# Engine order from a list scheduler, scores by head pair, transposes in the hT ring: a banded attention followed by a squared-ReLU MLP on one Trainium2 core

## Chip, cores, metric

One core of one Trainium2 chip. The metric is the device time of one execution in microseconds (us), the median of several runs. A "span" is the time from the first to the last instruction of the one profiled execution; it is some 1.8 us shorter than the same execution as timed (266.5 against 268.28 us for the kernel before).

Engines: PE does matmuls, PEld loads their stationary operand, DVE and ACT work on tensors, POOL issues most loads here (the prediction calls them SWDGE loads), SP the stores.

Names in the profiles: `tr`, `trq`, `trk`, `trx` are transposes on PE; `qz` is q transposed, with the two heads of a pair kept apart by zeros, `kT` is k transposed; `sc` are scores, `esc` their exp, `at` that times the mask; `po` is the attention output, `x` the same normalised, `xT` its transpose; `hT`, `hr`, `hs` are the hidden layer before the relu, after it, and squared; `acc` are the output accumulators and `o` the copy of one that is stored ("eviction"); `win` and `wout` are the weights. PE shows two rates here: eight `hT` matmuls last 1.04 us at the full rate and about 1.9 us at the half rate.

## The reference

```python
# q, k, v: (4, 8, 768, 64); n_global 8, n_local 96
scores = scale * q @ k.T + bias            # bias: -slope[h] * distance
keep   = is_global | is_local              # first 8 keys, and the last 96
a      = softmax(where(keep, scores, -1e9))
x      = (a @ v).transpose(0, 2, 1, 3).reshape(3072, 512)
out    = relu(x @ w_in) ** 2 @ w_out       # w_in (512, 2048), w_out (2048, 512)
```

There are 24 tiles of 128 rows, six per batch. As keys reach back 96 rows only, a tile needs its own keys and those of the tile before. Two tiles make a block of 256 rows for the MLP: 12 blocks, each in 8 steps of 256 hidden columns, 96 steps in all.

## The kernel before

All eight banks of PSUM, the buffers for matmul results, are used (the prediction cites the page for the number): two for the output accumulators `acc`, two for `hT`, two for one score tile `sc`, one for transposes `tr`, one for attention outputs `po`. The order of instructions on each engine is that in which Python emits them, by a hand-made table of times:

```python
def unit_a(j):                       # transposes of q and k, both into ONE bank
    if j < NPLAIN:                   # the two fp32 "plain" tiles: cast by DVE first
        nc.vector.tensor_copy(q_sb[j], plain["q", j])
        nc.vector.tensor_copy(k_sb[j], plain["k", j])
    tr = ps_tr.tile([P, 2 * NPAIR, P], BF16, name="tr", tag="tr")
    # ... four transposes of q, four of k
    nc.vector.tensor_copy(z[:D, :, 0, :], tr[:D, :NPAIR, :])
    nc.vector.tensor_copy(z[D:, :, 1, :], tr[D:, :NPAIR, :])
    nc.scalar.copy(kT[j], tr[:, NPAIR:, :])
# unit_scores: 4 matmuls into a tile of two banks, one exp and one multiply of 1024
# unit_pv: 8 small matmuls into po, then reciprocal and normalisation on DVE
# unit_f: 4 transposes of x into the tr bank, copied to xT by ACT

def stage1(g):                       # 8 matmuls into hT, relu on ACT, square on DVE
    ...
def stage2(g):                       # 4 matmuls into acc[0], acc[1]
    ...
    if s == NSTEP - 1:               # end of a block: evict and store
        for sub in range(2):
            nc.scalar.copy(o, acc[blk][sub])
            nc.sync.dma_start(out=out[r : r + P, :], in_=o)

put(0, A=-9, B=-8.9, D=-8.6, E=-8.4, F=-8.3)      # ... a line per early tile
for g in range(-1, NG + DELAY):
    if 0 <= g < NG:
        stage1(g)
    while pos < len(when) and when[pos][0] < g + 1:
        _, j, u = when[pos]
        UNITS[u](j)
        pos += 1
    if g - DELAY >= 0:
        stage2(g - DELAY)
```

The softmax here doesn't subtract the row's maximum and nothing guards it: scores larger than these inputs give would overflow.

## Time and profile before

| | before |
|---|---|
| time, median of 3 runs | 268.24 us |
| span of the profiled run | 266.5 us |
| PE stream (all matmuls by their start-to-start) | 212.3 us |
| first hT matmul | 26.7 us |
| PE idle for the o copy of a block | 10.5 us, 9 times |

The group lines read: source line, engine, operation, output <- inputs, shapes, count, then busy us and mean ns of one, then how long the engine stood idle just before these and for whom. The lines themselves stand in the prediction.

### The profile page before, as it was taken

To read this page: it belongs to the slowest core of one execution; us is meant where nothing else is said; L and a number is where in the kernel's file an instruction comes from. 1 tells how busy PE (TensorE), PEld (TensorE's weight loads), DVE (VectorE), ACT (ScalarE), POOL (GpSimd) and SP (SyncE) were. 2 spreads that over 40 slices of the span, in tenths; PEclk is the share of its full clock that TensorE was granted. 3 is DMA by queue.
4 is the path that set the end of the run, shared out by engine and by line. 5 is a ranking of instruction groups with operands and counts; after the bars stand their busy time and mean duration, and the time that the engine had idled before them with its cause. 6 is when DMAs were issued, how large, how long until landed. Compare 5 with 4: busy or idle time off the path is not lost.

```text
span 266.5 us, 4844 instructions
## 1 busy us (share of the span) xinstructions
PE 223.3 (84%) x1935; PEld 160.3 (60%) x1968; DVE 151.1 (57%) x350; ACT 139.8 (52%) x229; POOL 73.4 (28%) x94
## 2 busy tenths in 40 slices
PE   1345969686989899899799899898998998999993
PEld 1124657464666677577577677576676775766641
DVE  6444576466457576565557567565575675653310
ACT  5432474444557456556556555654745646635321
POOL 8986778999994000000000000000000000000000
PEclk9999999999999999999999999999999999999999
DMA  8999999999999300200200200200200200202022
GB/s 161 155 196 200 186 180 155 157 155 155 198 157 154 87 2 0 81 1 2 79 2 1 79 2 0 81 0 2 79 2 1 79 2 1 81 0 81 0 79 79
DMA packets 84758, 20.76 MB, mean 78 GB/s; under 512 B 75520, under 2 KB 81664, under 8 KB 84736
## 3 DMA queue, kind: packets, MB, share of 16 engines
q0 software_dynamic: 77120, 13.11, 63.2%
q1 hardware_dynamic: 7616, 7.34, 8.3%
q8 instruction: 15, 0.25, 0.4%
q14 instruction: 7, 0.06, 0.1%
HBM read 27.26 MB, written 6.29 MB: 126 GB/s over the span
## 4 chain that ended last, share of the span: by engine, by line
PE 66%; DVE 16%; ACT 11%; issue 5%; ACTq 0%
PE acc L338 27%; PE hT L314 26%; PE sc L219 7%; DVE hs L325 4%; ACT hr L323 4%; DVE x L275 3%; DVE qz L188 2%; ACT esc L228 2%; PE po L265 2%; ACT o L349 2%; PE trx L291 2%; DVE qz L187 2%; ACT kT L189 2%; DVE at L237 1%; DVE rs L274 1%
## 5 line engine op out<-in xcount | busy, mean ns | idle before, releaser
L325 DVE TENSOR_TENSOR hs<-hr 128x512 bf16<-128x512 f32 x96 | 66.3, 691 | 69.6 <-ACT hr L323 69.3
L338 PE MATMUL acc<-wout,hs 128*128 128x512 bf16 x351 | 92.9, 379 | 12.3 <-ACT o L349 10.5
L314 PE MATMUL hT<-xT,win 128*128 128x256 bf16 x768 | 101.2, 276 | 0.1
L314 PEld LDWEIGHTS <-win 128*128 128x128 bf16 x768 | 75.7, 99 | 28.2 <-issue 0.2
L323 ACT ACTIVATE hr<-hT 128x512 f32<-128x512 f32 x96 | 57.7, 601 | 54.6 <-PE hT L314 54.6
L338 PEld LDWEIGHTS <-hs 128*128 128x128 bf16 x384 | 35.7, 98 | 37.6 <-issue 13.2
L228 ACT ACTIVATE esc<-sc 128x1024 bf16<-128x1024 f32 x44 | 45.2, 1028 | 5.8 <-PE sc L219 4.7
L237 DVE TENSOR_TENSOR at<-esc,E 128x1024 bf16<-128x1024 bf16 x44 | 30.4, 691 | 27.1 <-ACT esc L228 27.0
L189 ACT COPY kT<-tr 128x512 bf16<-128x512 bf16 x24 | 14.0, 584 | 50.8 <-DVE qz L188 45.1
L219 PE MATMUL sc<-qz,kT 128*128 128x256 bf16 x160 | 25.8, 287 | 7.5 <-ACT kT L189 5.2
L87 POOL DMA_DIRECT2D v<-in_v_dram x24 | 23.4, 975 | 2.6 <-DMA win<-in_moe_w_in_dram 1.2
L96 POOL DMA_DIRECT2D k<-in_k_dram x22 | 21.3, 968 | 3.3 <-DMA wout<-in_moe_w_out_dram 2.8
L219 PEld LDWEIGHTS <-kT 128*128 128x128 bf16 x160 | 15.3, 102 | 10.6 <-ACT kT L189 6.1
L96 POOL DMA_DIRECT2D q<-in_q_dram x22 | 21.2, 965 | 1.4 <-DMA win<-in_moe_w_in_dram 0.7
L275 DVE TENSOR_TENSOR x<-po,rs 128x256 bf16<-128x256 f32 x48 | 20.4, 425 | 1.7
L265 PE MATMUL po<-v,at 128*128 128x65 bf16 x320 | 16.8, 196 | 3.4 <-DVE x L275 3.4
L265 PEld LDWEIGHTS <-at 128*128 128x128 bf16 x320 | 15.1, 100 | 5.7 <-DVE x L275 4.9
L349 ACT COPY o<-acc 128x512 f32<-128x512 f32 x24 | 13.0, 597 | 6.3 <-PE acc L338 6.3
L180 PE MATMUL tr<-ident,q 128*128 128x128 bf16 x96 | 9.9, 230 | 6.8 <-DVE q L175 6.8
L294 ACT COPY xT<-trx 128x512 bf16<-128x512 bf16 x24 | 14.0, 582 | 3.1 <-PE trx L291 3.1
L291 PE MATMUL trx<-ident,x 128*128 128x128 bf16 x96 | 9.9, 226 | 5.7 <-ACT kT L189 4.1
L291 PEld LDWEIGHTS <-x 128*128 128x128 bf16 x96 | 7.5, 100 | 6.9 <-issue 4.5
(34 smaller groups left out, 94.2 us busy)
## 6 DMA issues: line engine op xcount, KB each, us to landing
out_dram<-o SPq DMA_DIRECT2D x24, 256.0 KB, 2.2
v<-in_v_dram POOLq DMA_DIRECT2D x24, 128.0 KB, 6.1
q<-in_q_dram POOLq DMA_DIRECT2D x22, 128.0 KB, 5.9
k<-in_k_dram POOLq DMA_DIRECT2D x22, 128.0 KB, 6.0
win<-in_moe_w_in_dram POOLq DMA_DIRECT2D x8, 256.0 KB, 7.2
wout<-in_moe_w_out_dram POOLq DMA_DIRECT2D x8, 256.0 KB, 9.8
plain_q<-in_q_dram SPq DMA_DIRECT2D x2, 256.0 KB, 3.9
plain_k<-in_k_dram SPq DMA_DIRECT2D x2, 256.0 KB, 4.3
```

What stands on the lines that cost most here:

```text
L87: nc.gpsimd.dma_start(out=v_sb[j][:, :, :D], in_=v[b, :, t * P : (t + 1) * P, :].rearrange("h p d -> p h d"),)
L96: nc.gpsimd.dma_start(out=dst.rearrange("p (h d) -> p h d", h=H), in_=src[b, :, rows, :].rearrange("h p d -> p h d"),)
L219: nc.tensor.matmul(out=sc[:, pi, i * 2 * P : (i + 1) * 2 * P], lhsT=kT[kj][:, pair, :], rhs=z[:, pair, :, :], start=True, stop=True, skip_ ...
L228: nc.scalar.activation(out=esc, in_=sc.rearrange("p a b -> p (a b)"), func=Act.Exp, scale=scale)
L237: nc.vector.tensor_mul(at, esc, bias)
L265: nc.tensor.matmul(out=po[:, hi, :], lhsT=a4[:, hi // 2, i, hi % 2, :], rhs=v_sb[kj][:, h, :], start=(i == 0), stop=(i == 1), skip_group_c ...
L275: nc.vector.tensor_tensor(out=x[:, 4 * hf : 4 * hf + 4, :], in0=po[:, :, :D], in1=rs.to_broadcast([P, 4, D]), op=Alu.mult,)
L291: nc.tensor.transpose(out=trx[:, kt, :], in_=x[:, kt * P : (kt + 1) * P], identity=ident)
L314: nc.tensor.matmul(out=hT[:, c, :], lhsT=w_in_sb[s][:, kt, c * P : (c + 1) * P], rhs=xT[blk][:, kt, :], start=(kt == 0), stop=(kt == KM - ...
L323: nc.scalar.activation(hr, hT, Act.Relu)
L325: nc.vector.tensor_mul(hs, hr, hr)
L338: nc.tensor.matmul(out=acc[blk][sub], lhsT=hs[:, c, sub * P : (sub + 1) * P], rhs=w_out_sb[s][:, c, :], start=(s == 0 and c == 0), stop=(s ...
```

## The change

The intent is that PE never waits. The hand table goes; every piece of work is registered with its costs, dependencies and buffer rings, and a list scheduler emits all in the order in which they could start. Scores are made one head pair at a time, in two buffers of one bank. Transposes of q, of k and of x each take a bank out of the hT ring, which grows to three (those of the first two tiles take one of the accumulators' banks). Copies out of PSUM go to ACT or DVE, whichever is free earlier in the plan. The two plain tiles, the first two of q and k, are transposed in fp32 without a cast. Some buffers outside PSUM grow too (`qz` from 3 to 4, `hs` from 10 to 14), and the last block finishes one accumulator before the other.

```diff
+class Plan:
+    LAG = {"PE": 0.25, "ACT": 0.15, "DVE": 0.12, "SP": 2.6, "POOLQ": 2.5, "DMA": 0.0}
+    ...                              # picks the op and engine with the earliest start
-    DELAY = 8
+    NACC = 2
+    NQ, NKT, NQZ = 10, 2 * TPB, 4
-    ps_acc = ... bufs=1              # two tags
-    ps_h   = ... bufs=2
-    ps_sc  = ... bufs=1              # tiles of two banks
-    ps_tr  = ... bufs=1
+    ps_acc = ... bufs=NACC           # one tag
+    ps_h   = ... bufs=5 - NACC       # three, shared with the transposes
+    ps_sc  = ... bufs=2              # tiles of one bank
...
+    clock = [6.0]                    # assumed landing: 0.85 us a load, 1.3 a weight
-            nc.sync.dma_start(       # plain q and k
+    for n, src, eng in (("q", q, nc.sync), ("k", k, nc.scalar)):
+            eng.dma_start(
...
-    for j in range(NT):
-        nc.vector.memset(v_sb[j][:, :, D : D + 1], 1.0)
     (qz memsets, mask work)
+    for j in range(NT):
+        nc.vector.memset(v_sb[j][:, :, D : D + 1], 1.0)
...
-    for s in range(NSTEP):
-        load_w_in(s)
     for s in range(NSTEP):
+        load_w_in(s)
         load_w_out(s)
...
+                z = plan.op(("z", e_, j), {"DVE": 0.43, "ACT": 0.57}, emit_z,
+                            deps=[tr] + qz_users[zi], key=base + 0.1)
...
-    when.sort()                      # and the loop over steps
+    for o in plan.run():
+        if o["emit"]:
+            o["emit"](o["engine"])
```

## The prediction

> **What bounds the kernel now.** I read the page first (busy shares, slices, groups), then PE's waits by stretch, the chain of waits over one steady block, and the timeline of the start and of the end.
>
> ```profile
> span 266.5 us, 4844 instructions
> PE 223.3 (84%) x1935; PEld 160.3 (60%) x1968; DVE 151.1 (57%) x350; ACT 139.8 (52%) x229; POOL 73.4 (28%) x94
> ...
> PE   1345969686989899899799899898998998999993
> ...
> L338 PE MATMUL acc<-wout,hs 128*128 128x512 bf16 x351 | 92.9, 379 | 12.3 <-ACT o L349 10.5
> ```
>
> PE is the bound, but 84% is not its rate: matmuls overlap, so I price them by start-to-start. In the timeline eight hT matmuls run from 251.32 to 252.19 (0.866 us, 108 ns each) and four acc matmuls from 250.45 to 251.32 (216 ns each). In the same way four scores take 0.44 us (109 ns), four transposes 0.222 (55.5 ns), eight po 0.245 (31 ns). The stream alone needs: hT 768 x 0.1083 = 83.2; acc 384 x 0.2165 = 83.1; sc 176 x 0.109 = 19.2; transposes 288 x 0.0555 = 16.0; po 352 x 0.031 = 10.9. Sum 212.4 us. So 54 of the 266.5 us are not PE streaming. Where are they?
>
> The start. Before the first hT matmul PE has streamed only 32 transposes, 16 scores, 24 po, 4.3 us:
>
> ```profile
> 4.52 0.61 PE L180 MATMUL tr<-ident,q 128*128 128x128 bf16 x4 [4.52 <-DVE q L175]
> ...
> 11.98 0.61 PE L180 MATMUL tr<-ident,q 128*128 128x128 bf16 x4 [2.25 <-DVE q L175]
> ...
> 26.66 1.89 PE L314 MATMUL hT<-xT,win 128*128 128x256 bf16 x8
> ```
>
> The reader sees that tile 1's transposes wait until 11.98, though its data is there early (longest plain landing 4.8 us after an issue at 2.82): DVE casts it behind tile 0's work. The first hT stands at 26.66: 26.7 - 4.3 = 22.4 us lost. The end: the last acc matmul starts at 262.0, so ends near 262.4, and copy and store take 4.1 us. Left for the middle: 54.1 - 22.4 - 4.1 = 27.6 us. PE's waits from 94 to 226, then from 26.7 to 94:
>
> ```profile
> PE acc L338 <- ACT o L349: 9.0, 7, 1.4
> ```
>
> ```profile
> PE sc L219 <- ACT kT L189: 3.6, 4, 1.0
> PE po L265 <- DVE x L275: 2.6, 4, 1.2
> PE trx L291 <- ACT kT L189: 2.5, 2, 1.7
> PE sc L219 <- ACT esc L228: 1.4, 2, 1.1
> PE acc L338 <- ACT o L349: 1.2, 1, 1.2
> ```
>
> In the steady part one wait is all there is, once in a block of eight steps. The chain of waits at such a boundary shows what holds the eviction:
>
> ```profile
> 107.19 0.69 DVE hs L325
> 108.01 0.42 DVE x L275
> 108.43 0.32 DVE qz L187
> 108.77 0.44 DVE qz L188
> 109.49 0.28 issue
> 109.77 0.60 ACT o L349
> 110.41 1.08 PE acc L338 x4
> ```
>
> The o copy itself is 0.60 us, but on ACT's queue it stands behind the kT copy, which waits for both qz copies of DVE (they share its source bank), which wait behind hs and x. A cross-queue knot, not a lack of ACT or DVE time (52% and 57% busy). The acc starts at 110.41, 129.36, 148.75 give a block of 19.4 us (18.95 with a first tile). Its stream is 8 x 1.732 + 2 tiles x 2.03 = 17.9 (17.2): 1.5 to 1.7 us lost per block, of which 1.2 to 1.45 is this wait.
>
> **What the Trainium skill says.** "TensorE: Matmul & The Clock Gate", Back-to-back issue gap, gives N/2.4 + 2.5 ns warm: 109 and 216 ns for 256 and 512 columns; the trace agrees (108, 216). It also gives a loaded figure of 131 ns at 512, which this trace does not reach. Part 1 of that page has the array at half rate until about 3.4 us of sustained work. The page's clock row shows 9s throughout, but in the chain the first hT groups take 1.71 and 1.72 us for eight, against 0.87 later: the durations agree. "PSUM — Partial Sum Buffer", Specifications, gives 8 banks of 2 KiB per partition: before uses 2 acc + 2 hT + 2 sc + 1 tr + 1 po, after 2 + 3 + 2 + 1, full both times, so the third hT bank is paid with the tr bank. No view shows banks. "Perfetto Trace Analysis", DVE / Act Engine Instruction, says each instruction pays a fixed bubble: exp of 1024 takes 1028 ns and relu of 512 takes 601, so 427 per half and about 174 fixed (estimate from both rows).
>
> **The change part by part.** From the built order of both kernels, the number of PE matmuls is the same; the stream stays 212.4.
>
> 1. Scores in pairs. 44 exps become 80 of 512 and 16 of 256 columns: by the split above 80 x 0.60 + 16 x 0.39 = 54 instead of 45.2 us. The multiplies: 1024 bf16 take 691 ns as 512 fp32 do, so the halves cost about 0.42 (estimate): 80 x 0.42 + 16 x 0.29 = 38 instead of 30.4. With copies now spread (ACT gets 24 qz, 20 kT, 17 xT, 12 o; DVE 24 qz, 4 kT, 7 xT, 12 o), ACT comes to hr 57.7 + 54 + 73 copies x 0.58 = 42 + masks 5.5, about 160 us, DVE to about 165. Both under 70% of the new span. The price lies beside PE.
>
> 2. The block boundary. In the new order the two o copies are split between ACT and DVE, and between a block's last acc and the next block's first stand transposes, one hT group and one score pair: 0.22 + 0.87 + 0.22 = 1.3 us of PE work, over an eviction of 0.6. kT no longer shares a bank with q's transposes, so it doesn't wait for qz. The 1.2 to 1.45 us goes; I keep 0.3 a block for slips. Seven blocks from 91 to 226 gain about 8 us.
>
> 3. The start. fp32 transposes straight from the plain tiles, no cast; q and k issued on two queues; the score pairs pipeline through exp and multiply. Against it: the memsets of v now stand after four qz memsets (0.52 each), an identity copy and the mask work (1.0), so DVE reaches v's first memset near 4.8 us, and POOL's first v load, issued at 2.96 before, waits for it. All SWDGE loads shift by about 1.9 us. k of tile 3, issued at 8.38 before, now near 10.2, lands about 6 us later, at 16.3 (median of that row). Then, cold: transpose 0.6, po 0.5, norm 0.65, po 0.5, norm 0.65, trx 0.7, xT 0.5, and the queueing of tile 1's last exps: first hT near 21 us. By then PE has streamed 40 transposes, 20 scores and 24 po: 5.1 us. 207.3 remain (208.1 before). The start gains 26.7 - 21 - 0.8 = about 5 us.
>
> 4. The ramp. Loads now go win, wout in turn. The bytes up to the last wout are the same, and it landed at 41.65 before (a later k load waits for it there); at the queue's 1.4 us per weight and 0.7 per load this gives, shifted, q of tile 4 near 29, win 5 near 34.5, q of tile 5 near 36.6, win 7 near 42. PE, from 21, reaches these places near 28, 34, 36 and 43: about 2 us of waits. Before, the ramp (26.7 to 91) lost some 16 us: 27.6 less 7 x 1.5 and about 1 at the end. It has the 11.3 us of listed waits, the half clock (about 3), and drains. With three hT banks, two score buffers and o, qz, kT no longer in one knot I expect: half clock 2.5, loads 2, queue order 3.5 (ACT has 14 relus, 11 exps and 5 copies in these first 21 us of PE stream, 18 us, so it is tight there).
>
> 5. The end. The last block finishes one acc early, but the other still needs copy and store: 4.1 us stays.
>
> Sum: 21 + 207.3 + 8 (ramp) + 2.5 (steady) + 0.5 (last block) + 4.1 = 243.4 us of span, 1.7 more as timed (266.5 span, 268.24 timed): 245. The allowances are more likely too big than too small, as before's steady waits are almost one kind alone; I put 243.
>
> **The rivals.** (a) The bank ring turns into the new wait: 96 hT groups and 72 transposes take turns in three banks, seven takings per four steps. For it: a transpose's two copies may sit on two queues. Against: the tightest place, hT group after q and k transposes and four acc, has 1.5 us from the earlier group's end, over a relu of 0.60 plus 0.2 of drain. If wrong by 0.3 us a step: 96 x 0.3 = +29, no gain left. (b) ACT or DVE becomes the bound in the ramp or queues in fixed order wait on each other, since the scheduler's durations are guesses: +5 to 10, 250. (c) Late loads: the order was fixed on assumed landings some 3 us earlier than my estimate; PE stops in order. Against: PE too runs later. +3 to 5. (d) It runs as dense as planned with hardly a wait: 21 + 207.3 + 4 + 4.1 + 1.7 = 238, or 236 if the first hT comes at 19.
>
> **Range and chances.** 243 us; 236 (rival d) to 251 (b) eight times in ten. Within 2% (above 262.9) would need rival (a) at 0.2 us a step: chance 0.03; slower 0.01; faster 0.96.
>
> **What would show it.** Right: first hT at 20 to 22 us; L338's wait for the o copy all but gone; blocks of 17.9 to 18.3 us; ACT near 160 and DVE near 165 us busy; PE's waits gathered before 45 us. Wrong: hT or transposes waiting for relu or copies each step (a); PE waiting for exps or kT after 45 us (b); matmuls released by DMA (c).

## The result, and the profile after

The changed kernel takes 235.92 us (235.41 to 236.87, 4 runs) against 268.18 us. The ratio is 0.8798, interval 0.8761 to 0.8834: 12% faster. The forecast was 243 (236 to 251): the direction and most of the size were right, but the time fell just under the range.

The page of the changed kernel, its counterparts of the lines shown for before:

```profile
span 235.1 us, 4992 instructions
...
PE 219.5 (93%) x1968; PEld 159.1 (68%) x1968; DVE 153.8 (65%) x399; ACT 149.8 (64%) x282; POOL 73.8 (31%) x94
...
PE   1768699999999999999999999999999999999992
...
L629 PE MATMUL acc<-wout,hs 128*128 128x512 bf16 x384 | 101.1, 379 | 0.8 <-DVE hs L598 0.8
```

PE reads 9 in every slice from the sixth to the last but one, and the acc group's wait for the o copy is gone. ACT and DVE are busier, as foreseen (150 and 154 us). All waits of PE in the whole run (columns: who waited for whom, us in total, times, longest):

```profile
PE trq L327 <- DVE v L215: 4.8, 1, 4.8
PE hT L565 <- DMA win<-in_moe_w_in_dram: 1.9, 3, 1.4
PE trq L327 <- DMA q<-in_q_dram: 1.7, 3, 0.7
PE po L466 <- DVE x L492: 1.1, 2, 0.8
PE trq L327 <- DVE kT L266: 0.8, 1, 0.8
PE acc L629 <- DVE hs L598: 0.8, 2, 0.6
PE trk L327 <- DMA k<-in_k_dram: 0.2, 1, 0.2
PE trx L528 <- DVE x L492: 0.2, 1, 0.2
```

Before, the waits were 10.5 us for the o copy, 6.8 for the casts of q at the start, 5.2 for kT, 4.1 for kT again ahead of trx, and so on. Now the first line is the start of the program, and what the ramp has left are loads. A block boundary in the timeline of the changed kernel (start us, length, instruction; PE, then the two o copies), to set against the chain of waits shown in the prediction:

```profile
76.27 0.59 PE L629 MATMUL acc<-wout,hs 128*128 128x512 bf16 x2
76.70 0.38 PE L375 MATMUL sc<-qz,kT 128*128 128x256 bf16 x2
76.92 0.59 PE L629 MATMUL acc<-wout,hs 128*128 128x512 bf16 x2
77.35 0.39 PE L528 MATMUL trx<-ident,x 128*128 128x128 bf16 x4
77.57 1.04 PE L565 MATMUL hT<-xT,win 128*128 128x256 bf16 x8
78.45 0.38 PE L375 MATMUL sc<-qz,kT 128*128 128x256 bf16 x2
78.66 1.03 PE L629 MATMUL acc<-wout,hs 128*128 128x512 bf16 x4
...
76.90 0.59 ACT L264 COPY o<-acc 128x512 f32<-128x512 f32 x1
...
78.30 0.67 DVE L266 COPY o<-acc 128x512 f32<-128x512 f32 x1
```

The old block's last acc pairs stand at 76.27 and 76.92, the new block's first at 78.66. Nothing is idle between (an idle stretch would stand in brackets). PE has 1.3 us of other work there. The first copy ends at 77.49, long before its accumulator is used again at 78.66; the second ends at 78.97, just before the pair that needs it (at about 79.1).

**Lost time.** One measure serves for all runs below. I count PE's stream in program order, every matmul at its start-to-start from the prediction, and subtract it from the real start of an hT group of eight. The difference is what PE has lost by then. Example: the changed kernel's first hT starts at 18.86, with 5.14 us of stream before it, so 13.7 are lost. "Ramp" is from the 1st to the 25th group (three blocks), "steady" from there to the 96th.

| kernel | time | first hT | lost: start | ramp | steady |
|---|---|---|---|---|---|
| before | 268.2 | 26.66 | 22.4 | 14.6 | 12.4 |
| changed | 235.9 | 18.86 | 13.7 | 3.8 | 0.3 |

So the 31.4 us of span come from the start (8.7), the ramp (10.8) and the steady part (12.1), less 0.2 after the last hT.

### The profile page after: what moved, and what is told of

Its sections match the earlier page's. It is cut to its first block, busy times and chain, and to the rows that moved or that the text cites. A ratio compares the mean times of both kernels' runs of the same rounds, so it can differ in the third digit from the quotient of the medians.

```text
span 235.1 us, 4992 instructions
## 1 busy us (share of the span) xinstructions
PE 219.5 (93%) x1968; PEld 159.1 (68%) x1968; DVE 153.8 (65%) x399; ACT 149.8 (64%) x282; POOL 73.8 (31%) x94
## 4 chain that ended last, share of the span: by engine, by line
PE 85%; DMA 6%; POOL 3%; DVE 3%; issue 1%; ACT 1%; POOLq 0%
PE hT L565 35%; PE acc L629 33%; PE sc L375 7%; DMA win<-in_moe_w_in_dram 4%; PE po L466 4%; DMA k<-in_k_dram 2%; PE trx L528 2%; PE trk L327 2%; PE trq L327 2%; POOL v L177 2%; DVE qz L196 1%; POOL q L177 1%; DVE x L492 1%; POOL k L177 0%; DVE hs L598 0%
## 5 line engine op out<-in xcount | busy, mean ns | idle before, releaser
L629 PE MATMUL acc<-wout,hs 128*128 128x512 bf16 x384 | 101.1, 379 | 0.8 <-DVE hs L598 0.8
L565 PE MATMUL hT<-xT,win 128*128 128x256 bf16 x768 | 98.4, 273 | 1.9 <-DMA win<-in_moe_w_in_dram 1.9
L403 ACT ACTIVATE esc<-sc 128x512 bf16<-128x512 f32 (+1 forms) x96 | 52.8, 558 | 5.0 <-PE sc L375 4.4
L423 DVE TENSOR_TENSOR at<-esc,E 128x512 bf16<-128x512 bf16 (+1 forms) x96 | 37.4, 392 | 0.5 <-ACT esc L403 0.3
L375 PE MATMUL sc<-qz,kT 128*128 128x256 bf16 x176 | 34.5, 277 | 0.2
L491 DVE RECIPROCAL rs<-po 128x4 f32<-128x4 f32 x48 | 8.7, 181 | 30.2 <-PE po L466 29.8
L264 ACT COPY qz<-trq 64x512 bf16<-64x512 bf16 x23 | 13.3, 580 | 5.1 <-DVE qz L266 2.9
L266 DVE COPY qz<-trq 64x512 bf16<-64x512 bf16 x21 | 8.8, 418 | 6.7 <-PE trq L327 5.8
L264 ACT COPY kT<-trk 128x512 bf16<-128x512 bf16 x20 | 11.7, 586 | 1.2 <-PE trk L327 0.7
L264 ACT COPY xT<-trx 128x512 bf16<-128x512 bf16 x17 | 10.0, 589 | 1.3 <-PE trx L528 1.0
```

The source lines that it names most:

```text
L264: nc.scalar.copy(dst, src)
L375: nc.tensor.matmul(out=sc[:, i, :], lhsT=kT[(j - i) % NKT][:, pair, :], rhs=qz[zi][:, pair, :, :], start=True, stop=True, skip_group_check ...
L403: nc.scalar.activation(out=esc[:, :n], in_=sc.rearrange("p a b -> p (a b)")[:, :n], func=Act.Exp, scale=scale,)
L423: nc.vector.tensor_mul(at_, tiles.pop(("esc", j, pair))[:, : at_.shape[1]], bias)
L565: nc.tensor.matmul(out=hT[:, c, :], lhsT=w_in_sb[s][:, kt, c * P : (c + 1) * P], rhs=tiles["xT", blk][:, kt, :], start=(kt == 0), stop=(kt ...
L629: nc.tensor.matmul(out=tiles["acc", blk, sub], lhsT=hs[:, c, sub * P : (sub + 1) * P], rhs=w_out_sb[s][:, c, :], start=(s == 0 and c == 0) ...
```

## The experiments

Theories. "Order": the gain comes from the order on the queues, above all from undoing a knot in which o and kT copies wait behind the qz copies. Rival "banks": the third hT bank and the double score buffer carry it. Further, why each allowance of the forecast was too large. "Before" took 268.1 to 269.4 us.

**1. Before, second stage first** (label b1_evict_early)

```diff
         stage1(g)
+        if g - DELAY >= 0:
+            stage2(g - DELAY)
         while pos < len(when) and when[pos][0] < g + 1:
             ...
-        if g - DELAY >= 0:
-            stage2(g - DELAY)
```

> The kernel before with one edit: in each step the second MoE stage is emitted ahead of the attention units, so at a block's end ACT gets the o copies before the kT copy. Theory 'queue knot': the 1.2 to 1.45 us wait per boundary (9 of them, 10.5 us) goes nearly away, the time falls by 8 to 11 us to about 258. Rival 'the eviction itself' (the acc banks are single, so the next block's first acc has to wait about 0.9 us after the last one whatever the queue): at most 3 us fall, about 265.

Measured: 254.43 us, ratio 0.9459 (0.9411 to 0.9508). Moving two lines gives 14 us. The group line of the acc matmuls in this run:

```profile
L338 PE MATMUL acc<-wout,hs 128*128 128x512 bf16 x384 | 98.3, 382 | 0.3 <-ACT o L349 0.3
```

10.5 us of waiting are 0.3 now, although the accumulators are still single: the eviction itself fits between two uses, and only its place on ACT's queue was wrong. Steady loss falls from 12.4 to 0.3, ramp from 14.6 to 12.8. The gain exceeds the upper end expected (11): that was drawn from the listed waits (10.5 us), while the start-to-start measure finds 12.1 us gained in the steady part alone, and 1.8 in the ramp. ACT's queue at a boundary, before and then in this run:

```profile
109.28 0.58 ACT L189 COPY kT<-tr 128x512 bf16<-128x512 bf16 x1 [2.13 <-DVE qz L188]
109.77 1.08 ACT L349 COPY o<-acc 128x512 f32<-128x512 f32 x2
...
103.85 1.10 ACT L349 COPY o<-acc 128x512 f32<-128x512 f32 x2
106.29 0.59 ACT L189 COPY kT<-tr 128x512 bf16<-128x512 bf16 x1 [1.35 <-DVE qz L188]
```

The first two lines belong to the boundary of the prediction's chain. The o copies now start 0.8 us after the block's last acc matmuls (103.08), where it was 2.5 us (107.26). The edit also moves these matmuls ahead of the attention units on PE; that part was not tried alone.

**2. to 4. The changed kernel on the banks of before**

a1_tr_bank: two hT banks, all transposes in one bank.

```diff
-    ps_h = ... bufs=5 - NACC
+    ps_h = ... bufs=2
+    ps_tr = ... bufs=1               # ("tr", 1, users) in the plan
```

> The changed kernel with the banks of before for hT and transposes: two hT banks, one bank for all transposes, schedule worked out anew. Theory 'order': the list order hides the tighter ring, at most 3 us slower than 235.9, below 239. Rival 'banks': the third hT bank carries much of the gain, 8 us slower or more, with hT or transposes waiting for copies in every step.

a2_wide_scores: two head pairs in one tile.

```diff
-    ps_sc = ... bufs=2;  for pair in range(NPAIR): ... exp and multiply of 512
+    ps_sc = ... bufs=1;  for hf in range(2): ... exp and multiply of 1024
```

> The changed kernel with the scores as before: two head pairs in one tile of two banks, one buffer, one exp of 1024 columns, schedule worked out anew. Theory 'order': at most 3 us slower than 235.9; ACT about 8 us and DVE about 7 us less busy, as 44 exps replace 96. Rival 'banks': score matmuls wait for the exp of the tile before, 0.3 us per tile or more, 8 us slower or more.

a12_order_only: both.

> Both undone at once: the list scheduler on the bank layout of before. Theory 'order': still below 243, that is at least 25 of the 32 us gained come from the order and the start alone. Rival 'banks': above 250.

Measured: 236.3, 235.15 and 235.25 us (ratios 0.8786, 0.8754, 0.8776, against 0.8798 for the changed kernel; all intervals overlap). With the banks of before the list order is as fast. (q's and k's transposes still are two tiles that take the one bank in turn; before they were one tile.) "Banks" is out, and so is my rival (a), since even two hT banks and one transpose bank make no step wait: steady loss is 0.3 in all three. The wide scores do make ACT less busy, 128.5 us against 149.8, and it is worth nothing, as ACT was not the bound. Here the expectation missed: of these 21 us only 7 are the exps (8 were expected for all); most of the rest are copies that the plan now gave to DVE, which got 8.5 us busier instead of 7 less.

**5. Before, second stage first and split banks** (b6_split_banks)

```diff
-    tr = ps_tr.tile([P, 2 * NPAIR, P], BF16, name="tr", tag="tr")
+    tr  = ps_h.tile([P, NPAIR, P], BF16, name="trq", tag="hT")   # ring of three
+    trk = ps_h.tile([P, NPAIR, P], BF16, name="trk", tag="hT")
...
-    nc.scalar.copy(kT[j], tr[:, NPAIR:, :])
+    nc.scalar.copy(kT[j], trk)
...                                  # x's transposes take from the ring of three too
```

> The kernel before with the second stage ahead of the units (254.4 us) and further with q's and k's transposes in banks of their own out of a ring of three hT banks, so that the kT copy doesn't wait for the two qz copies. Theory 'the knot of kT and qz costs the ramp too': the 12.8 us lost between the first hT and the 24th group fall to 9 or less, 3 to 5 us faster, about 250. Rival 'hand order': scores stand on PE right behind their transposes, so that a wait remains whichever copy comes first; at most 1.5 us faster.

Measured: 246.96 us, ratio 0.9197 (0.9155 to 0.9239), 7.5 us below run 1 (6.0 between the two profiled runs). Ramp loss falls from 12.8 to 8.6, the first hT comes at 24.86. More than expected: banks matter in the hand order and don't in the list order. The edit splits the shared bank and adds a third hT bank at once, so which of the two helps is not separated. Part of the fall is PE's rate: run 1 has a stretch at the half rate in its ramp (granted clock 0.50 from 65.8 to 69.2 us) that this run has not.

**6. The same with early casts** (b65_early_casts)

```diff
-    if j < NPLAIN: cast tile j       # tile 1's casts behind tile 0's multiply
+    if j == 0: cast tile 0
     ...
+    if j == 0: cast tile 1           # right after tile 0's qz and kT copies
```

> The last hand-ordered kernel (second stage first, split banks, 247.0 us, first hT at 24.86) with both plain tiles' casts issued on DVE right after tile 0's qz copies, instead of behind tile 0's multiply. Theory 'the cast order makes the late start': tile 1's transposes move from 11.9 to about 9, the first hT moves 2 us or more earlier, time about 245. Rival 'the start is a chain of single waits on every engine': first hT less than 1 us earlier.

Measured: 245.23 us, ratio 0.9146. Tile 1's transposes move from 12.11 to 9.53, the first hT from 24.86 to 22.85, 2 us as expected. The hand order with three small edits has 23 of the 32 us.

**7. Before with dummy matmuls** (b3_dummy_matmuls)

```diff
+    if (j, u) in ((0, "F"), (1, "D"), (1, "E"), (1, "F"), (2, "B")):
+        # four matmuls of 512 columns, ident x q_sb[0], result not read
```

> The kernel before with 20 dummy matmuls of 512 columns in PE's gaps of the start (ahead of five units between 18 and 26 us; their result is not read). Theory 'a denser PE brings the full clock': the first two groups of eight hT matmuls take 0.87 us instead of 1.71, the time falls by 1 to 2 us if the dummies themselves don't delay the start. Rival 'the half rate at 26 us is not a matter of density': the groups stay at 1.7 us and the time rises by up to 3 us.

Measured: 269.05 us, ratio 1.0032 (0.999 to 1.0073): the same. The timeline of this run:

```profile
18.63 1.90 PE L383 MATMUL warm<-q,ident 128*128 128x512 bf16 x4
...
21.95 1.03 PE L383 MATMUL warm<-q,ident 128*128 128x512 bf16 x3
...
27.15 1.04 PE L314 MATMUL hT<-xT,win 128*128 128x256 bf16 x8
...
34.22 1.56 PE L314 MATMUL hT<-xT,win 128*128 128x256 bf16 x8
...
36.85 1.60 PE L314 MATMUL hT<-xT,win 128*128 128x256 bf16 x8
```

The dummies do bring the full rate: four take 1.90 us first and 1.03 later (of the group shown as x3 one has no record), and the first hT group, 1.89 us before, takes 1.04. Yet the end doesn't move. The first hT is 0.5 us later; at the third group this kernel is 1.2 us ahead (30.48 against 31.69), and by the sixth it is 0.4 behind. In between the half rate comes back: the granted clock is 0.50 from 34.6 to 38.0, and the groups there take 1.56 and 1.60 us. PE had been busy for 1.56 of the 3.4 us before that, with no wait over 1.02. So this run moves the half rate rather than removing it, and doesn't tell what it costs.

**8. Changed kernel with casts** (a3_casts)

```diff
-    identity=ident32, fp32 transposes of the plain tiles
+    DVE casts to bf16, bf16 transposes
```

> The changed kernel with the two plain tiles cast to bf16 by DVE and transposed as bf16, as before, instead of fp32 transposes. Theory 'fp32 transposes keep PE busy and so bring the full clock early': the first hT groups run at half rate again (1.7 us for eight instead of 0.87) or the full rate comes some us later than the 11.7 us seen, and the first hT stands 1 us or more later for the casts; 1.5 to 3 us slower. Rival 'the clock follows the denser start whatever the transposes are': full rate before the first hT, at most 1 us slower.

Measured: 235.54 us, ratio 0.8765 (0.8729 to 0.88): the same as the changed kernel or a little less, first hT at 18.40. In its timeline four transposes take 0.63 us at 12.70 and 0.39 at 14.13, so the full rate comes at about 14 us instead of the 11.7 of the changed kernel, still ahead of the first hT. The rival is right: the fp32 transposes are not needed for it, and they are no source of the gain.

**9. Memsets of v first** (a4_v_memset_first)

```diff
+    for j in range(NT):
+        nc.vector.memset(v_sb[j][:, :, D : D + 1], 1.0)
     nc.vector.tensor_copy(ident32, ident)
     (qz memsets, mask work)
-    (memsets of v)
```

> The changed kernel with the memsets of v ahead of those of qz on DVE, as before. Theory 'the loads of POOL are late by the memset wait' (first v load at 4.55, before at 2.96): loads are issued 1.5 us earlier, q of tile 3 and k of tile 3 land 1 to 1.5 us earlier, first hT near 17.7, 1 us faster or a little more. Rival 'DMA engines are full from the plain loads on': landings hardly move, no change (within 0.4 us).

Measured: 234.37 us, ratio 0.8724 (0.8692 to 0.8756). The size was expected, the place wasn't:

```profile
10.27 1.09 PE L327 MATMUL trk<-ident,plain_k 128*128 128x128 f32 x4 [1.10 <-issue]
...
19.12 1.03 PE L565 MATMUL hT<-xT,win 128*128 128x256 bf16 x8
```

The loads of POOL start at 2.97 instead of 4.55, but the first hT is no earlier (19.12): PE now waits ahead of tile 1's k transposes (10.27, against 8.81 before the edit). The profile names no releaser for that wait, but the trace has PE's semaphore instruction ahead of it, which takes 2.32 us (7.89 to 10.21). Of the two semaphores in it, the load's was complete at 7.86; DVE's was raised at 10.18, at the end of tile 1's second qz copy:

```profile
8.78 1.39 DVE L266 CAST qz<-trq 64x512 bf16<-64x512 f32 x2 [1.21 <-PE trq L327]
```

In the changed kernel the same transposes wait for the load alone. So PE stood for DVE's copies; why this build waits for them is not shown. What the earlier loads save are the waits of the ramp: its loss falls from 3.8 to 0.7, with the order of instructions on PE, ACT and DVE unchanged.

**10. Corrected landing times** (a5_landings)

```diff
-    clock = [6.0]      # 0.85 a load, 1.3 a weight
+    clock = [8.2]      # 0.9 a load, 1.6 a weight
```

> The changed kernel with the scheduler's assumed landing times moved to what the trace shows (start 8.2 instead of 6.0 us, 0.9 instead of 0.85 a load of q, k, v, 1.6 instead of 1.3 a weight). Theory 'wrong landing times cost waits in the ramp': the 3.8 us lost between the first hT and the 24th group fall to about 2.5, 1 to 1.5 us faster. Rival 'there is no other work to do at that point': same within 0.5 us.

Measured: 236.05 us, ratio 0.8776: no change. PE waits for no DMA any more, but the order that respects the landings starts hT 0.6 us later and waits for exps and copies instead (ramp loss 2.8). The plan's landing times were some 4 to 5 us too early for the weights, and correcting them gained nothing.

**11. No allowances in the plan** (a6_no_lags)

```diff
-    LAG = {"PE": 0.25, "ACT": 0.15, "DVE": 0.12, ...
+    LAG = {"PE": 0.0, "ACT": 0.0, "DVE": 0.0, ...
```

> The changed kernel with the scheduler's allowances for semaphore and drain time set to zero (PE 0.25, ACT 0.15, DVE 0.12 us before), so that each engine's queue is ordered as if results were there at once. Theory 'queues are loose, as ACT and DVE are under 70% busy': same within 2 us in all, losses only in the ramp. Rival 'queue order is fragile' (my rival b): the steady part loses 0.3 us a step, 10 us or more slower.

Measured: 238.53 us, ratio 0.8892 (0.8859 to 0.8924). Steady loss rises from 0.3 to 3.4 us over 71 steps, 0.05 a step: real, but a sixth of what rival (b) asked. The allowances are worth 2.6 us.

**12. Wide scores, transpose bank, memsets of v first** (a412_best)

```diff
-    the changed kernel's ps_h, ps_sc, place of the v memsets
+    those of runs 2, 3 and 9
```

> Best guess: the list order with wide scores and the transpose bank (as the order-only run, 235.25) plus the memsets of v first (234.37 alone). Theory 'the two gains are separate': start 13.9 and ramp about 1 us lost, 233.5 us. Rival 'the ramp gain is the same loads' waits, already partly gone in the order-only kernel' (ramp 2.6 there): 234.3.

Measured: 235.07 us, ratio 0.8756. No better than its parts: the ramp loses 0.9, but the first hT comes at 20.99, against 19.27 in run 4. The order on PE, ACT and DVE is that of run 4, as the memsets are not in the plan. But the wait of run 9 stands here too (a semaphore instruction of 2.31 us; tile 1's k transposes at 10.20 against 8.79), and PE stays at the half rate longer: four transposes still take 0.63 us at 17.95, and 0.38 at 12.36 in run 4.

**13. to 15. On one chip: the changed kernel, the best version, one queue**

a0_after_again is the changed kernel unedited. a43_casts_memset:

```diff
-    fp32 transposes of the plain tiles; memsets of v last
+    the casts of run 8; memsets of v first, as in run 9
```

a8_one_queue:

```diff
-    (("q", q, nc.sync), ("k", k, nc.scalar))
+    (("q", q, nc.sync), ("k", k, nc.sync))
```

> The changed kernel itself, unedited, so that the others of this group are compared with it on one chip: 235.9 us expected.

> The changed kernel with both edits that were not slower: bf16 casts in place of fp32 transposes (235.54) and the memsets of v first (234.37). Theory 'the first hT is held by the plain tiles' landing, and the earlier loads save ramp waits only': first hT 18.4 to 19.1, ramp loss under 1.5 us, time 234 to 234.5. Rival 'casts free the start to use the earlier loads': first hT near 17.5, 233.

> The changed kernel with the four plain loads all issued from SP's queue, as before, instead of q on SP and k on ACT. Theory 'two queues matter little, as the transfers share the same bandwidth': within 0.5 us. Rival 'issuing in parallel makes the early start': k of tile 1 lands 1 us later, first hT later by as much, 1 us slower.

Measured: 235.75, 234.08 and 235.82 us; ratios 0.8785 (0.8758 to 0.8813), 0.8726 (0.8699 to 0.8752) and 0.8795. The version with both edits is 0.7% faster than the changed kernel on the same chip, the intervals just apart, and it beats both kernels. Its first hT is at 19.07 and its ramp loses 0.8, as its theory said (that the plain tiles' landing holds the first hT is not shown by this). Its full rate comes only between 16.0 and 17.2 us, and no cost of that shows in the time. The second queue matters nothing: issued one after the other on SP, the plain loads land in a median of 4.0 and 4.5 us from issue, against 5.0 and 5.4 on two queues, and the last of the four lands at 7.8 us against 7.6.

All runs by the measure of lost time:

| run | time | first hT | start | ramp | steady |
|---|---|---|---|---|---|
| b1_evict_early | 254.4 | 26.66 | 22.4 | 12.8 | 0.3 |
| b6_split_banks | 247.0 | 24.86 | 20.6 | 8.6 | 0.3 |
| b65_early_casts | 245.2 | 22.85 | 18.6 | 7.4 | 0.3 |
| b3_dummy_matmuls (dummies not counted as stream) | 269.1 | 27.15 | 22.9 | 14.2 | 12.4 |
| a1_tr_bank | 236.3 | 18.74 | 13.6 | 3.3 | 0.3 |
| a2_wide_scores | 235.2 | 19.20 | 13.8 | 2.9 | 0.3 |
| a12_order_only | 235.3 | 19.27 | 13.9 | 2.7 | 0.3 |
| a3_casts | 235.5 | 18.40 | 13.3 | 2.7 | 0.3 |
| a4_v_memset_first | 234.4 | 19.12 | 14.0 | 0.7 | 0.3 |
| a5_landings | 236.1 | 19.48 | 14.1 | 2.8 | 0.3 |
| a6_no_lags | 238.5 | 18.70 | 13.8 | 2.4 | 3.4 |
| a412_best | 235.1 | 20.99 | 15.6 | 0.9 | 0.3 |
| a43_casts_memset | 234.1 | 19.07 | 13.9 | 0.8 | 0.3 |
| a8_one_queue | 235.8 | 18.72 | 13.6 | 3.0 | 0.3 |
| a0_after_again | 235.8 | 18.78 | 13.6 | 3.1 | 0.3 |

## Why the prediction was right and wrong

The mechanism was right. What failed is the size of three terms of the sum: the ramp (8 us allowed, 3.8 lost), the start (first hT at 21, measured 18.86) and the boundaries (2.5, measured 0.3).

**What bounds the kernel** was right. PE's stream of 212.3 us is the floor, and the changed kernel's losses add up to its span: 212.3 + 13.7 + 3.8 + 0.3 + 0.9 after the last hT + 4.1 for the last copy and store = 235.1.

**Step 2, the boundary,** had the right mechanism, shown by run 1: the o copy stood behind the kT copy. Its allowance of 0.3 us a block, 2.5 us in all, was too large: measured, 0.3 us in all. This term failed by 2.2 us.

**Step 3, the start,** put the first hT at 21; it came at 18.86, 2.1 us earlier. The shift of POOL's loads was real (first v load at 4.55, forecast 4.8), but two things in the step failed. The landing of tile 3's k, on whose transposes PE stood in its program order, took 5 us from issue, not the 6 of the row's median over the whole run: issued at 9.89, its transposes ran at 14.85. And the rest of the chain took 4.0 us, not 4.7, partly because it ran at full rate, where I had taken half-rate lengths:

```profile
10.72 0.61 PE L327 MATMUL trq<-ident,q 128*128 128x128 bf16 x4 [0.42 <-DMA q<-in_q_dram]
...
11.71 0.39 PE L327 MATMUL trk<-ident,k 128*128 128x128 bf16 x4
...
14.85 0.40 PE L327 MATMUL trk<-ident,k 128*128 128x128 bf16 x4 [0.22 <-DMA k<-in_k_dram]
...
18.86 1.03 PE L565 MATMUL hT<-xT,win 128*128 128x256 bf16 x8
```

Run 9 doesn't settle how much the landing alone holds: the k of tile 3 lands at 13.29 there, but PE, held earlier by DVE, reaches its transposes only at 15.06. From them to the first hT it is 4.1 us again.

**Step 4, the ramp,** was the largest miss: 8 us allowed, 3.8 lost. Of its three terms, the half clock (2.5) was nothing: PE was at the full rate from 11.7 us on, before the first hT. The prediction carried over a loss of before, where the first two groups of eight took 1.89 and 1.91 us instead of 1.04 and four scores 1.06 instead of 0.60, about 2.2 us. The queue order (3.5) left little besides: once run 9 brings the loads earlier, in the same order, the ramp loses 0.7 in all, so about 3 of the 3.8 were loads. The term for loads (2) was therefore somewhat too small; the listed waits on DMA after the first hT (1.9 for win, 0.7 for q) come near those 3.

**The sum** came to 245, 9.1 us over the measured 235.9: 2.1 from the start, 4.2 from the ramp, 2.2 from the boundaries, 0.9 from timed less span (1.7 assumed; the profiled run was the slowest of the four, so its span is only 0.8 under the median), less 0.4 in the last block.

**Steps 1 and 5** held. Exps of 512 columns took 594 ns and those of 256 took 381, as split beforehand (0.60 and 0.39 us). ACT and DVE got busier (149.8 and 153.8 us, some 10 below the forecast of 160 and 165) without any cost to PE, shown by run 3, and the end stayed 4.1 us. The last block lost 0.9, forecast 0.5.

**The rivals.** (a) and (b) did not happen; run 2 and run 11 put bounds on both. (c) was half right: loads are what the ramp still waits for. (d), "238, or 236 if the first hT comes at 19", is what happened. I gave it too little weight: each step but the loads got its own allowance on the pessimistic side, and the lower end of the range then sat at the best case instead of below it.

**Where the gain came from.** Measured one edit after the other on the kernel before: 14 us from putting the second stage, with the eviction, first; 7.5 from splitting q's and k's bank together with the third hT bank; 1.7 from the cast order. The other 9 us, 4.9 of them in the start and 3.6 in the ramp, come with the list kernel; in the steady part it adds nothing to run 1, which loses the same 0.3. About 0.7 of the 3.6 is PE's rate: the first hT group of run 6 took 1.73 us, that of the changed kernel 1.03. Banks, fp32 transposes, the second queue and the landing times are excluded as their cause by runs 2 to 4, 8, 15 and 10. Which of its placements earns them is not isolated: the split of copies between ACT and DVE, the order of the weight loads and the deeper rings of `qz` and `hs` were not tried alone.

## What to carry to other kernels

When the bound engine waits although the others are half idle, look at what stands ahead of the releaser on its own queue, not at the releaser's length: an eviction of 0.60 us cost about 1.4 us per block (12.1 us over 8.9 blocks) because of its place, and moving two lines gave 14 of 32 us before any buffer was touched. When forecasting, ask of each loss of before whether the change leaves it in place (here the half rate was over ahead of the first hT), and don't add a safety allowance to every step of a sum.

## What the Trainium skill lacked or had wrong

- "TensorE: Matmul & The Clock Gate", Back-to-back issue gap: the loaded figure of 131 ns per 512-column matmul is not met here; in the steady part of all kernels the start-to-start is 216 ns, which its formula for the isolated gap gives.
- The same page, Part 1: the penalty of the half rate is given as extra time of the whole. Ahead of the first hT, where PE waits a lot, it doesn't show as that: with the full rate from 16.2 us on (run 2, another order) instead of 11.7 the first hT came at 18.74 instead of 18.86; in run 14 the full rate came over 4 us later than in the changed kernel and the time was lower. Run 7 can't test it for the ramp, as the half rate came back there.
- The same page, Part 4, says that transposes don't bring the full clock in the way matmuls do. In the changed kernel PE had done little but transposes (16 in fp32, 4 in bf16, with six score matmuls and four po) when it reached full rate at about 11.7 us; with bf16 casts (run 8) it took until about 14 us. No run separates the transposes from the rest.
- No page gives the time of a 128x128 fp32 transpose: four took 0.88 us start to start (4.75 to 5.63) at the half rate, 220 ns each.
- "PSUM — Partial Sum Buffer", Terms, says that engines are to be kept apart per bank, but no page says what sharing one bank between two readers can cost through the queues: splitting q's and k's transposes, with a third hT bank, gave 7.5 us in the hand order (run 5); in the list order one bank for all transposes, taken in turn, cost nothing (run 2).
